# One transposition for the last 64 channels of two token tiles, two folded modulation vectors, and another order of the first operations

## The chip, the cores and the metric

The kernel runs on one core of one Trainium2 chip. The metric is the device time of one execution in microseconds, the median of several runs. The engines that a reader meets below are PE (TensorE, the matrix engine, with its weight loads listed apart as PEld), DVE (VectorE), ACT (ScalarE), POOL (GpSimd) and SP (SyncE, which here only issues loads and stores). Each engine runs its own instructions in program order and waits on semaphores for the others.

## The reference

The block has two halves. `x` is 2048 tokens of 448 channels. Six modulation vectors come from `silu(c) @ w_mod`.

```python
mod = (silu(c) @ w_mod).reshape(1, 6, 1, -1)
sa, ca, ga, sb, cb, gb = (mod[:, i] for i in range(6))
h = layernorm(x) * (1 + ca) + sa
qkv = h @ wqkv                       # 16 heads of 28 channels
pq, pk = phi(q), phi(k)              # phi(t) = where(t > 0, t + 1, exp(t)) + 1e-6
kv = einsum("bhsd,bhse->bhde", pk, v);  z = pk.sum(tokens)
num = einsum("bhqd,bhde->bhqe", pq, kv)
den = einsum("bhqd,bhd->bhq", pq, z)[..., None] + 1e-6
x = x + ga * ((num / den) @ wo)
h = layernorm(x) * (1 + cb) + sb
u = gelu(einsum("bsd,sf->bdf", h, w1) + b1)      # over tokens: 2048 -> 1792
x = x + gb * transpose(einsum("bdf,fs->bds", u, w2) + b2)
```

## The kernel before, in words

Tokens are cut into 16 tiles of 128, channels into three chunks of 128 and a last one of 64. Full precision is kept by splitting an operand into a high part (rounded, float32r) and a low part (the remainder): a product is hi x hi, hi x lo and lo x hi, three matmuls of 448 columns. The last chunk has only 64 rows, so its high and low parts lie one above the other in one operand of 128 rows. High parts are copies on ACT, low parts subtractions on DVE.

There is no scheduler: `tc.manual_schedule()` leaves the order of every engine's queue to the order of the calls in the source.

The stages, with the names that are used later:

- Start, about 0 to 22 us. SP issues the loads: transposed tiles `xt`, weights `wr`, the first two modulation weights `wt` (`wfirst`), tiles `x`. `keep_warm` gives PE matmuls on a constant, whose result nobody reads, until the first weights are there. `col_sum` (DVE) makes the scale (1 + ca) and the shift sa as columns; `w_high` and `w_low` make the weights with the scale folded in, `wh` and `wl`. `row_part` (DVE, tile `accb`) adds up the row bias that the shift gives, `row_sum` and `row_bias` (PE, bank `rowb`) sum it over partitions, and `row_out` writes it to the row operand `wrow`. The mean and variance of tiles 0 and 1 are made on ACT (`a_stats_act`, tile `as`) and finished on POOL (`mv`, `ve`, a power); those of later tiles begin on DVE. `a_rows` and `a_transpose` (`rowst`, bank `rw`) turn the means into a row of the moving operand. The projection `kp` of a tile is ended by `close`, one matmul with `wrow`.
- The loop for k and k^T x, t = 4 to 15, to about 100 us: projections `kp`, `a_exp` (`ek`, `rk`), `a_pk` (phi(k)), `a_pk_parts` (its high and low parts, and its sum over tiles, which a DMA issued by POOL accumulates), `a_outer` (banks `cacc`); some of the q projections are made early. The modulation vectors three to five are summed on DVE (`mod_part`), split (`mod_split`), and summed over partitions and spread by PE with a matrix of ones (`mod_sum2`, bank `modp`), 112 rows at a time.
- About 100 to 114 us: the sum of phi(k), kv, and its product with `wo` (`wp`), which is split into `Wph` and `Wpl`.
- The loop over token tiles, about 114 to 212 us, `for i in range(NT + LAG)`. In step i PE transposes phi(q)/den of tile i (`b_transpose`, `pn` to the bank `tq`), multiplies tile i - 1 (`b_out`, bank `op`, with the parts `pth` and `ptl` that `b_high`, `b_low` and `b_low_last` make of `tq`), and does the first twelve matmuls of the token MLP for tile i - 5 (`step`, banks `up`). DVE adds `op` to x (`b_res`, tile i - 2), prepares `pn` of tile i + 1 (`b_prod`, `b_sum`, `b_eps`, `b_recip`, `b_scale`), normalises and makes low parts.
- The rest of the token MLP, `up` to about 300 us and `y` to about 432 us.

Pools: 74 slots and 27 token slots of 512 columns in SBUF, 8 PSUM banks of 512 columns.

Of the kernel before, what the change touches and what calls it, by code (L numbers as in the profile page):

```python
# [8 lines left out]
F32 = mybir.dt.float32  # L9
# [5 lines left out]
P = 128  # L15
# [27 lines left out]
POOL_LOW = (0, 2)  # L43
PRE = 9
MID = 5
NSLOT, NTOK = 74, 27
# [5 lines left out]
def block_kernel(ctx: ExitStack, tc: tile.TileContext, x, xt, wqkv, wo, w1, b1, w2, b2, c, wmod, wfirst, out):  # L52
# [176 lines left out]


    def mod_split(j):
        acc = macc.pop(j)
        macc[j] = (moving(slot, f"mh{j}", parts=G), moving(slot, f"ml{j}", parts=G))
        split(acc, *macc[j])

    def mod_sum2(j):
        ps = bank(f"modp{j}")
        hi, lo = macc.pop(j)
        nc.tensor.matmul(ps[:, :D], ones_r[:G, :], hi, start=True, stop=False)
        nc.tensor.matmul(ps[:, :D], ones_r[:G, :], lo, start=False, stop=True)  # L240
        return ps
# [99 lines left out]
    def a_stats_act(ts):  # L341
        n = len(ts)
        g, ve = a_group(ts)
        sm = small.tile([P, n, 3], F32, name=f"as{ts[0]}", tag=f"as{n}")

        def one(i):
            t, s3 = ts[i], sm[:, i, :]
            nc.scalar.activation(junk, X[t], AF.Identity, accum_out=s3[:, 0:1])
            nc.scalar.activation(s3[:, 1:2], s3[:, 0:1], AF.Copy, scale=-1.0 / D)
            b_square(X[t], s3[:, 1:2], s3[:, 2:3], f"s{t}")  # L350

        def end():
            nc.gpsimd.tensor_scalar_mul(g[:, :, 0:1], sm[:, :, 0:1], 1.0 / D)
            nc.gpsimd.tensor_scalar(ve, sm[:, :, 2:3].to_broadcast([P, n, 2]), 1.0 / D, EPS,
                                    op0=ALU.mult, op1=ALU.add)
            a_pow(g, ve)
            groups[ts[0]] = g
        return one, end
# [137 lines left out]
    def a_pk_parts(t):  # L496
# [14 lines left out]
        pks[t] = (hi, lo)  # L511


    cacc = []
# [16 lines left out]
    spread()  # L531
    keep_warm(4)
    nc.scalar.activation(sel_s, sel_f, AF.Copy)
# [49 lines left out]
    end23()  # L583
    a_split_high(5)
    row_out(1)
    a_transpose(0)
    a_copy(0)
# [9 lines left out]
    load_xt(10)  # L597
    load_x(10)
    a_exp(0, kps[0])
    a_high(0)  # L600
# [20 lines left out]
    low()  # L621
    a_split(6)
    a_transpose(4)
# [18 lines left out]
    a_pk_parts(2)  # L642
    low()
    a_split(7)
    wo_sb = []
    late = [t for t in range(NT) if t not in Q_EARLY.values()]
    for t in range(4, NT):
# [53 lines left out]
        if pair:  # L701
            second(1)
            end()
        if 4 <= t < 8:
            w_high(0, t - 4)
            if t == 7:
                w_row(0)
# [82 lines left out]

    dens, prods = {}, {}

# [14 lines left out]
    def b_scale(t):  # L807
        pn = tslot(f"pn{t}")
        nc.vector.scalar_tensor_tensor(pn.rearrange("p (h d) -> p h d", d=DH),
                                       pq[t].rearrange("p (h d) -> p h d", d=DH), 1e-6,  # L810
# [5 lines left out]
    def b_transpose(t):  # L816
        pn = pns.pop(t)
        tps[t] = bank(f"tq{t}")
        for ch in range(3):
            nc.tensor.transpose(tps[t][:, ch * P:(ch + 1) * P], pn[:, ch * P:(ch + 1) * P], ident)  # L820
        nc.tensor.transpose(tps[t][:64, 384:], pn[:, 384:D], ident)
# [10 lines left out]
    def b_low_last(t):  # L832
        ps, hi = tps.pop(t), phs[t][0]
        nc.vector.tensor_sub(hi[64:, 384:], ps[:64, 384:], hi[:64, 384:].bitcast(F32))

    def b_out(t):
        ph, pl = phs.pop(t)
        opb[t] = bank(f"op{t}")
        todo = []
        for ch in range(3):  # L840
            s = slice(ch * P, (ch + 1) * P)
            todo += [(ph[:, s], Wph[ch]), (ph[:, s], Wpl[ch]), (pl[:, s], Wph[ch])]
        todo += [(ph[:, 384:], Wph[3]), (ph[:, 384:], Wpl[3])]
        for n, (a, b) in enumerate(todo):
            nc.tensor.matmul(opb[t][:, :D], a, b, start=(n == 0), stop=(n == len(todo) - 1))  # L845

# [85 lines left out]
    for i in range(NT + LAG):  # L932
# [4 lines left out]
        if i == NT:  # L937
            mod_split(5)
        if i < NT:
            b_transpose(i)  # L940
# [376 lines left out]
```

## Time and profile before

| | |
|---|---|
| Time, median of 3 runs | 437.97 us (437.96 to 438.0) |
| Profiled execution | 438.01 us |
| Its span | 436.3 us |
| Instructions | 7203 |
| PE busy | 429.2 us (98%) |
| DVE busy | 360.6 us (83%) |
| ACT busy | 275.3 us (63%) |
| POOL busy | 117.9 us (27%) |

The span is the time from the first to the last instruction in the trace; the execution around it is 1.7 us longer. In the rows that are quoted below, "kp<-wh,hh" names the output and the inputs of an instruction, "128x448" its elements (partitions x columns), x3 how often it stands there; a group of rows with the same line, engine and shape can be one row. Times that matmuls end are modelled, so consecutive matmuls overlap in the rows and their pitch is the distance of their starts.

### The profile page before, as it was taken

How to read it: one execution, taken by the hardware profiler on the slowest of the kernel's cores; microseconds unless marked ns; L12 is line 12 of the kernel's file. 1: busy time of each engine (PE TensorE's matmuls, PEld its weight loads, DVE VectorE, ACT ScalarE, POOL GpSimd, SP SyncE). 2: the span in 40 equal slices, each digit the busy share in tenths (PEclk: the TensorE clock that was granted, in tenths of full speed). 3: DMA queues.
4: the chain of work that ended last, by engine and by line, in shares of the span. 5: the costliest groups of instructions: out<-in, count | busy, mean ns of one | idle time of the engine just before them, and what ended most of it. 6: DMA issues, size and time to landing. Idle time of an engine off the chain costs nothing.

```text
span 436.3 us, 7203 instructions
## 1 busy us (share of the span) xinstructions
PE 429.2 (98%) x2337; PEld 398.8 (91%) x2337; DVE 360.6 (83%) x809; ACT 275.3 (63%) x587; POOL 117.9 (27%) x200
## 2 busy tenths in 40 slices
PE   8899999999999999999999999999999999999996
PEld 8688899999899999999999999999999999999996
DVE  4899986689799999994679695829799988898894
ACT  5689867749657798886756263537464565645550
POOL 4335454100024477773300000010113131132010
PEclk9999999999999999999999999999999999999999
DMA  8997998465300036335417561587379977985430
GB/s 273 382 338 154 228 230 200 80 193 180 124 2 0 26 66 152 74 74 139 152 65 223 178 209 45 148 213 218 71 171 235 201 173 156 223 180 119 83 54 32
DMA packets 63941, 66.14 MB, mean 152 GB/s; under 512 B 4960, under 2 KB 55456, under 8 KB 63904
## 3 DMA queue, kind: packets, MB, share of 16 engines
q1 hardware_dynamic: 54832, 50.90, 37.6%
q0 software_dynamic: 8784, 14.32, 20.9%
q10 hardware_dynamic: 288, 0.46, 0.5%
q8 instruction: 18, 0.29, 0.3%
q14 instruction: 19, 0.16, 0.1%
HBM read 46.30 MB, written 7.34 MB: 123 GB/s over the span
## 4 chain that ended last, share of the span: by engine, by line
PE 89%; DVE 3%; DMA 2%; ACT 2%; POOL 1%; issue 1%; SPq 1%; DVEq 0%; ACTq 0%; POOLq 0%
PE y L1112 19%; PE up L897 10%; PE up L896 10%; PE up L895 10%; PE y L1113 9%; PE op L845 8%; PE qp L419 7%; PE cacc L525 6%; PE kp L419 3%; PE tq L820 1%; DMA wr<-in_qkv_dram 1%; DMA x<-in_A_x_dram 1%; PE qp L426 1%; PE kvb L776 1%; DVE st L367 1%
## 5 line engine op out<-in xcount | busy, mean ns | idle before, releaser
L896 PE MATMUL up<-h2l,ph 128*128 128x448 f32 x224 | 81.3, 363 | 0.0
L897 PE MATMUL up<-h2h,pl 128*128 128x448 f32 x224 | 81.2, 363 | 0.0
L895 PE MATMUL up<-h2h,ph 128*128 128x448 f32 x224 | 80.8, 361 | 0.0
L1067 POOL DMA_DIRECT2D a<-a x16 | 14.2, 959 | 138.0 <-DMA a<-in_B_w_dram 77.1
L896 PEld LDWEIGHTS up<-h2l,ph 128*128 128x128 f32 x224 | 42.0, 188 | 3.3 <-DVE h2l L892 0.3
L895 PEld LDWEIGHTS up<-h2h,ph 128*128 128x128 f32 x224 | 41.9, 187 | 3.0
L897 PEld LDWEIGHTS up<-h2h,pl 128*128 128x128 f32 x224 | 42.0, 188 | 2.5
L84 DVE TENSOR_TENSOR pl<-pr,ph 128x512 fp32r<-128x512 f32 x46 | 30.7, 685 | 4.2 <-ACT ph L83 3.3
L1118 ACT ACTIVATE cc<-y 128x448 f32<-128x448 f32 x24 | 13.0, 547 | 26.8 <-PE y L1113 26.8
L83 ACT ACTIVATE ph<-pr 128x512 fp32r<-128x512 f32 x46 | 27.6, 625 | 0.8 <-PE up L897 0.5
L1031 DVE TENSOR_TENSOR u<-u,mod 128x448 f32<-128x448 f32 x14 | 8.7, 621 | 21.6 <-ACT u L1030 21.4
L419 PE MATMUL kp<-wh,hh 128*128 128x448 f32 x64 | 24.4, 386 | 0.2 <-ACT rk L436 0.2
L845 PE MATMUL op<-wph,pth 128*128 128x448 f32 x64 | 24.5, 383 | 0.0
L1030 ACT ACTIVATE u<-up,b1c 128x448 f32<-128x448 f32 x14 | 8.8, 627 | 24.0 <-PE up L897 23.5
L1132 POOL DMA_DIRECT2D out_dram<-yt x14 | 12.7, 910 | 40.5 <-DVE yt L1123 31.1
L525 PE MATMUL cacc<-pkh,xh 128*128 128x448 f32 x64 | 23.6, 369 | 0.0
L419 PE MATMUL qp<-wh,hh 128*128 128x448 f32 x64 | 23.4, 366 | 0.0
L845 PE MATMUL op<-wpl,pth 128*128 128x448 f32 x64 | 23.1, 361 | 0.0
L802 POOL TENSOR_SCALAR den<-den 128x16 f32<-128x16 f32 x16 | 8.8, 549 | 43.6 <-DVE den L799 43.6
L525 PE MATMUL cacc<-pkl,xh 128*128 128x448 f32 x56 | 20.3, 362 | 0.0
L1073 DVE TENSOR_TENSOR a<-a,s 128x512 f32<-128x512 f32 (+1 forms) x32 | 18.5, 619 | 0.0
L1112 PE MATMUL y<-ub,a11h 128*128 128x448 f32 x56 | 18.2, 375 | 0.0
(233 smaller groups left out, 1362.3 us busy)
## 6 DMA issues: line engine op xcount, KB each, us to landing
pr<-in_B_w_dram SPq DMA_DIRECT2D x56, 256.0 KB, 3.0
a<-in_B_w_dram SPq DMA_DIRECT2D x32, 256.0 KB, 4.6
a<-in_B_w_dram SPq DMA_DIRECT2D x32, 192.0 KB, 4.6
xt<-in_xt_dram SPq DMA_DIRECT2D x16, 256.0 KB, 5.0
x<-in_A_x_dram SPq DMA_DIRECT2D x16, 224.0 KB, 5.0
wm<-in_B_wmod_dram SPq DMA_DIRECT2D x16, 196.0 KB, 4.9
out_dram<-x SPq DMA_DIRECT2D x14, 224.0 KB, 2.4
out_dram<-yt POOLq DMA_DIRECT2D x14, 224.0 KB, 5.5
```

The source lines that it names most:

```text
L83: nc.scalar.activation(hi, full, AF.Copy)
L84: nc.vector.tensor_sub(lo, full, hi.bitcast(F32))
L419: nc.tensor.matmul(pps[t, j][:, :D], a[:, ch * P:(ch + 1) * P], w, start=first, stop=False)
L525: nc.tensor.matmul(cacc[ch][:, :D], a[:, s], b, start=(t == 0 and i == 0), stop=(t == NT - 1 and i == len(todo) - 1))
L845: nc.tensor.matmul(opb[t][:, :D], a, b, start=(n == 0), stop=(n == len(todo) - 1))
L895: nc.tensor.matmul(ps[:, :D], hi[:, sl], mh, start=first, stop=False)
L896: nc.tensor.matmul(ps[:, :D], hi[:, sl], ml, start=False, stop=False)
L897: nc.tensor.matmul(ps[:, :D], lo[:, sl], mh, start=False, stop=last)
L1067: nc.gpsimd.dma_start(w, a, accum_op=ALU.add)
L1073: nc.vector.tensor_tensor(w, raw2[q, a][i], raw2[q, b][i], op=op)
L1112: nc.tensor.matmul(ps[:, :D], h[:, s], w, start=opens and r == 0, stop=False, skip_group_check=True)
L1113: nc.tensor.matmul(ps[:, :HD], l[:, s], wh, start=False, stop=closes and r == PAIRS - 1, skip_group_check=True)
```

## The change

It has four parts.

**Transposition.** `pn` gets a slot of 512 columns. The transposition of an even tile leaves out its last 64 channels; ACT copies them beside the last 64 of the next tile (`b_beside`), and the odd tile's fourth transposition turns both at once, 128 columns. High and low parts of the last chunk of both tiles are then made in the odd step, across partitions where needed. The two matmuls of an even tile with its last chunk (`b_out_last`) move to the start of the step after the next one, ahead of its transposes.

PE in the loop over token tiles, before: the end of a step and the next one (ph and pl are parts of W1, h2h and h2l of the normalised tile).

```order
L897 MATMUL up3_1924<-h2h1_1952,pl1_1350 128x448
L820 MATMUL tq7_2062<-ident_78,pn7_2049 128x128 x3
L821 MATMUL tq7_2062<-ident_78,pn7_2049 64x128
L845 MATMUL op6_2067<-wph0_1610,pth6_2012 128x448
...
L845 MATMUL op6_2067<-wph3_1622,pth6_2012 128x448
L845 MATMUL op6_2067<-wpl3_1623,pth6_2012 128x448
L895 MATMUL up0_1921<-h2h2_2027,ph2_1396 128x448
...
L897 MATMUL up3_1924<-h2h2_2027,pl2_1397 128x448
L820 MATMUL tq8_2138<-ident_78,pn8_2125 128x128 x3
```

And after, the step of tile 8 and the beginning of that of tile 9:

```order
L937 MATMUL up3_1922<-h2h2_2029,pl2_1399 128x448
L885 MATMUL op6_2067<-wph3_1622,pth6_2013 128x448
L885 MATMUL op6_2067<-wpl3_1623,pth6_2013 128x448
L848 MATMUL tq8_2140<-ident_78,pn8_2125 128x128 x3
L878 MATMUL op7_2144<-wph0_1610,pth7_2089 128x448
...
L885 MATMUL op7_2144<-wpl3_1623,pth7_2089 128x448
...
L937 MATMUL up3_1922<-h2h3_2101,pl3_1403 128x448
L848 MATMUL tq9_2212<-ident_78,pn9_2171 128x128 x4
```

The last two matmuls of op6 now stand behind the up matmuls of the step before and ahead of the transposes of tile 8; the odd tile has four whole transposes.

DVE in the same loop, after, from the parts of tile 7 to those of tile 8 (before, each tile had one L834 row, the low part of its own last chunk, between L805 and L809):

```order
L863 TENSOR_TENSOR ptl7_2090<-tq7_2062,pth7_2089 128x384
L831 RECIPROCAL den8_2111<-den8_2111 128x16
L870 TENSOR_TENSOR pth6_2013<-tq7_2062,pth6_2013 64x128
L870 TENSOR_TENSOR pth7_2089<-tq7_2062,pth7_2089 64x128
L835 SCALAR_TENSOR_TENSOR pn8_2125<-pq8_1683,den8_2111 128x448
L932 TENSOR_TENSOR h2l3_2102<-y3_2037,h2h3_2101 128x448
L894 SCALAR_TENSOR_TENSOR x6_170,sm6_2173<-op6_2067,x6_170 128x448
L821 SCALAR_TENSOR_TENSOR pd9_2175<-pq9_1685,zb_1380 128x448
...
L863 TENSOR_TENSOR ptl8_2169<-tq8_2140,pth8_2168 128x384
L831 RECIPROCAL den9_2190<-den9_2190 128x16
L835 SCALAR_TENSOR_TENSOR pn9_2171<-pq9_1685,den9_2190 128x448
```

The two low parts of the last chunks of tiles 6 and 7 stand together ahead of pn8; the residual sum of tile 6 stands where it stood, and its op6 now ends two matmuls into PE's step of tile 8.

**Folding.** For the third and sixth modulation vectors (j = 2 and 5) DVE first adds the upper 48 of the 112 rows to the lower ones; the 64 rows that are left are split into a high and a low half of one operand of 128 rows, and PE needs one matmul instead of two.

**Start.** `x` of tile 0 is issued ahead of the four loads of the first modulation weights and `x` of tile 1 between them; `keep_warm` runs seven instead of four; the column sums and row parts alternate, without the low part of tile 3 between them; the mean and variance of tiles 0 and 1 are finished on DVE (their power stays on POOL); the low part of tile 4 stands behind `wrow`, and the high part of tile 6 ahead of the first exponential.

DVE in the start, before, from the first column sum of the shift (wt_0_138) to wrow's predecessors:

```order
L220 SCALAR_TENSOR_TENSOR wt_0_138,col_202<-wt_0_138,scr 128x449
L220 SCALAR_TENSOR_TENSOR wt_1_141,col_202<-wt_1_141,scr 128x449
L220 SCALAR_TENSOR_TENSOR wt_2_144,col_202<-wt_2_144,scr 128x449
L220 SCALAR_TENSOR_TENSOR wt_3_147,col_202<-wt_3_147,scr 64x449
L265 TENSOR_SCALAR accb_309<-wr_0_117,col_202 128x448
L402 TENSOR_TENSOR hl_301<-xt_154,hh_300 128x512
L267 SCALAR_TENSOR_TENSOR accb_309<-wr_1_122,col_202,accb_309 128x448
L267 SCALAR_TENSOR_TENSOR accb_309<-wr_2_129,col_202,accb_309 128x448
L267 SCALAR_TENSOR_TENSOR accb_309<-wr_3_134,col_202,accb_309 128x448
L402 TENSOR_TENSOR hl_316<-xt_156,hh_315 128x512
L382 CAST rowst_104<-mv_282 128x4x2
```

And after:

```order
L222 SCALAR_TENSOR_TENSOR wt_0_140,col_202<-wt_0_140,scr 128x449
L222 SCALAR_TENSOR_TENSOR wt_1_143,col_202<-wt_1_143,scr 128x449
L282 TENSOR_SCALAR accb_293<-wr_0_117,col_202 128x448
L284 SCALAR_TENSOR_TENSOR accb_293<-wr_1_122,col_202,accb_293 128x448
L222 SCALAR_TENSOR_TENSOR wt_2_148,col_202<-wt_2_148,scr 128x449
L222 SCALAR_TENSOR_TENSOR wt_3_151,col_202<-wt_3_151,scr 64x449
L284 SCALAR_TENSOR_TENSOR accb_293<-wr_2_129,col_202,accb_293 128x448
L284 SCALAR_TENSOR_TENSOR accb_293<-wr_3_134,col_202,accb_293 128x448
L370 TENSOR_SCALAR mv_285<-as_287 128x2
L371 TENSOR_SCALAR ve_286<-as_287 128x4
L419 TENSOR_TENSOR hl_315<-xt_154,hh_314 128x512
L399 CAST rowst_104<-mv_285 128x4x2
```

The low part of tile 3 (hl of xt_154) has left the row parts, mv and ve have come behind them, and the low part of tile 4 (hl of xt_156) is no longer ahead of rowst.

**Sums.** The DMA that adds phi(k) of a tile to the running sum is issued at the end of the step (`sum_end`), behind the statistics' power on POOL and not ahead of it.

The diff, cut:

```diff
+FOLDED = (2, 5,)
...
     load_xt(2)
+    load_x(0)
     for ch in range(4):
+        if ch == 2:
+            load_x(1)
         load_first(0, ch)
-    load_x(0)
-    load_x(1)
...
+    def halves(acc, new, name):
+        n = acc.shape[0] - 64
+        nc.vector.tensor_add(acc[:n], acc[:n], acc[64:])
+        both = moving(new, name)
+        nc.scalar.activation(both[:64], acc[:64], AF.Copy)
+
+        def low():
+            nc.vector.tensor_sub(both[64:], acc[:64], both[:64].bitcast(F32))
+        return both, low
...
     def mod_sum2(j):
         ps = bank(f"modp{j}")
-        hi, lo = macc.pop(j)
-        nc.tensor.matmul(ps[:, :D], ones_r[:G, :], hi, start=True, stop=False)
-        nc.tensor.matmul(ps[:, :D], ones_r[:G, :], lo, start=False, stop=True)
+        part = macc.pop(j)
+        for i, m in enumerate(part):
+            nc.tensor.matmul(ps[:, :D], ones_r[:m.shape[0], :], m, start=(i == 0), stop=(i == len(part) - 1))
         return ps
...
         def end():
-            nc.gpsimd.tensor_scalar_mul(g[:, :, 0:1], sm[:, :, 0:1], 1.0 / D)
-            nc.gpsimd.tensor_scalar(ve, sm[:, :, 2:3].to_broadcast([P, n, 2]), 1.0 / D, EPS,
+            nc.vector.tensor_scalar_mul(g[:, :, 0:1], sm[:, :, 0:1], 1.0 / D)
+            nc.vector.tensor_scalar(ve, sm[:, :, 2:3].to_broadcast([P, n, 2]), 1.0 / D, EPS,
...
         elif t in SUM_DMA:
-            nc.gpsimd.dma_start(pksum[t % 2], pk, accum_op=ALU.add)
+            late_sum.append((pksum[t % 2], pk))
...
-    keep_warm(4)
+    keep_warm(7)
...
-    for ch in range(4):
+    for ch in (0, 2):
         col_sum(0, ch)
+        col_sum(0, ch + 1)
+        row_part(1, ch)
+        row_part(1, ch + 1)
     row_sum(1)
-    a_split_high(3)
     act01(1)
     end01()
-    row_part(1, 0)
-    a_split_low(3)
-    for ch in (1, 2, 3):
-        row_part(1, ch)
-    a_split(4)
+    a_split(3)
     projects(in_turn(3)[:4], 1, "kp")
     row_bias(1)
     projects(in_turn(3)[4:], 1, "kp")
+    a_split_high(4)
+    a_split_high(5)
...
-    a_split_high(5)
     row_out(1)
+    a_split_low(4)
...
+    a_split_high(6)
     a_exp(0, kps[0])
...
     def b_transpose(t):
         pn = pns.pop(t)
         tps[t] = bank(f"tq{t}")
-        for ch in range(3):
+        if t % 2 == 0:
+            lasts[t] = pn
+        for ch in range(3 + t % 2):
             nc.tensor.transpose(tps[t][:, ch * P:(ch + 1) * P], pn[:, ch * P:(ch + 1) * P], ident)
-        nc.tensor.transpose(tps[t][:64, 384:], pn[:, 384:D], ident)
+
+    def b_beside(t):
+        pns[t + 1] = tslot(f"pn{t + 1}", w=512)
+        nc.scalar.activation(pns[t + 1][:, D:], lasts.pop(t)[:, 384:D], AF.Copy)
 
     def b_high(t):
...
-        nc.scalar.activation(phs[t][0][:64, 384:], tps[t][:64, 384:], AF.Copy)
+        if t % 2:
+            for i, s in ((t, slice(0, 64)), (t - 1, slice(64, P))):
+                nc.scalar.activation(phs[i][0][s, 384:], tps[t][s, 384:], AF.Copy)
...
     def b_low_last(t):
-        ps, hi = tps.pop(t), phs[t][0]
-        nc.vector.tensor_sub(hi[64:, 384:], ps[:64, 384:], hi[:64, 384:].bitcast(F32))
+        ps = tps.pop(t)
+        if t % 2:
+            for i, s, o in ((t - 1, slice(64, P), slice(0, 64)), (t, slice(0, 64), slice(64, P))):
+                hi = phs[i][0]
+                nc.vector.tensor_sub(hi[o, 384:], ps[s, 384:], hi[s, 384:].bitcast(F32))
...
+    def b_out_last(t):
+        ph = phs.pop(t)[0]
+        for b in (Wph, Wpl):
+            nc.tensor.matmul(opb[t][:, :D], ph[:, 384:], b[3], start=False, stop=(b is Wpl))
...
+        if i % 2 == 0 and 0 < i <= NT:
+            b_out_last(i - 2)
         if i < NT:
             b_transpose(i)
...
             b_high(i)
+            if i % 2 == 0:
+                b_beside(i)
```

More of the change, by code (lines that the diff above doesn't have):

```diff
@@ L228, in mod_part @@
             nc.vector.scalar_tensor_tensor(macc[j], wm[j, k], sc[:G, k:k + 1], macc[j], op0=ALU.mult, op1=ALU.add)
+    def halves(acc, new, name):
[6 more added lines that the diff above has]
+        return both, low
     def mod_split(j):
         acc = macc.pop(j)
-        macc[j] = (moving(slot, f"mh{j}", parts=G), moving(slot, f"ml{j}", parts=G))
-        split(acc, *macc[j])
+        if j in FOLDED:
+            both, low = halves(acc, slot, f"mh{j}")
+            low()
+            macc[j] = (both,)
+        else:
+            macc[j] = (moving(slot, f"mh{j}", parts=G), moving(slot, f"ml{j}", parts=G))
+            split(acc, *macc[j])
     def mod_sum2(j):
         ps = bank(f"modp{j}")
-        hi, lo = macc.pop(j)
-        nc.tensor.matmul(ps[:, :D], ones_r[:G, :], hi, start=True, stop=False)
-        nc.tensor.matmul(ps[:, :D], ones_r[:G, :], lo, start=False, stop=True)
+        part = macc.pop(j)
+        for i, m in enumerate(part):
+            nc.tensor.matmul(ps[:, :D], ones_r[:m.shape[0], :], m, start=(i == 0), stop=(i == len(part) - 1))
         return ps
@@ L511, in a_pk_parts, with sum_end @@
         pks[t] = (hi, lo)
+    late_sum = []
+    def sum_end():
+        while late_sum:
+            nc.gpsimd.dma_start(*late_sum.pop(0), accum_op=ALU.add)
     cacc = []
@@ L621, in block_kernel @@
     low()
-    a_split(6)
+    a_split_low(6)
     a_transpose(4)
@@ L643, in block_kernel @@
     low()
+    sum_end()
     a_split(7)
@@ L703, in block_kernel @@
             end()
+        sum_end()
         if 4 <= t < 8:
@@ L789, in block_kernel @@
     pns, phs, ys, opb, sums, nms, nm2s, rss, vss = {}, {}, {}, {}, {}, {}, {}, {}, {}
-    dens, prods = {}, {}
+    dens, prods, lasts = {}, {}, {}
     def b_prod(t):
@@ L807, in b_scale @@
     def b_scale(t):
-        pn = tslot(f"pn{t}")
-        nc.vector.scalar_tensor_tensor(pn.rearrange("p (h d) -> p h d", d=DH),
+        pn = pns.pop(t, None) or tslot(f"pn{t}", w=512)
+        nc.vector.scalar_tensor_tensor(pn[:, :D].rearrange("p (h d) -> p h d", d=DH),
                                        pq[t].rearrange("p (h d) -> p h d", d=DH), 1e-6,
@@ L832, in b_low_last @@
     def b_low_last(t):
-        ps, hi = tps.pop(t), phs[t][0]
-        nc.vector.tensor_sub(hi[64:, 384:], ps[:64, 384:], hi[:64, 384:].bitcast(F32))
+        ps = tps.pop(t)
[3 more added lines that the diff above has]
+                nc.vector.tensor_sub(hi[o, 384:], ps[s, 384:], hi[s, 384:].bitcast(F32))
     def b_out(t):
-        ph, pl = phs.pop(t)
+        ph, pl = phs[t]
         opb[t] = bank(f"op{t}")
-        todo = []
         for ch in range(3):
             s = slice(ch * P, (ch + 1) * P)
[L842 to L845, printed above, removed]
+            for n, (a, b) in enumerate(((ph[:, s], Wph[ch]), (ph[:, s], Wpl[ch]), (pl[:, s], Wph[ch]))):
+                nc.tensor.matmul(opb[t][:, :D], a, b, start=(ch == n == 0), stop=False)
+        if t % 2:
+            b_out_last(t)
+    def b_out_last(t):
+        ph = phs.pop(t)[0]
+        for b in (Wph, Wpl):
+            nc.tensor.matmul(opb[t][:, :D], ph[:, 384:], b[3], start=False, stop=(b is Wpl))
     def b_sums(i):
```

## The prediction

> **What bounds the kernel now.** I read the page first, then TensorE's waits, then the chain of the first 45 us, then the timelines of the two places that the change touches. The page's lines on busy time and on the granted clock:
>
> ```profile
> span 436.3 us, 7203 instructions
> PE 429.2 (98%) x2337; PEld 398.8 (91%) x2337; DVE 360.6 (83%) x809; ACT 275.3 (63%) x587; POOL 117.9 (27%) x200
> PEclk9999999999999999999999999999999999999999
> ```
>
> TensorE (PE) is busy for 98% of the span, at an open clock in every slice. So a matmul taken away is worth its pitch, and other engines cost something only where PE waits. TensorE's whole list of waits has five rows; four matter (us in total, times, longest):
>
> ```profile
> PE rowb L277 <- DVE accb L267: 1.6, 1, 1.6
> PE kp L426 <- DVE wrow L282: 0.5, 1, 0.5
> PE kp L419 <- ACT rk L436: 0.2, 1, 0.2
> PE rw L391 <- DVE rowst L385: 0.2, 1, 0.2
> ```
>
> That is 2.5 us. The chain of waits shows where (start, us, engine):
>
> ```profile
> 9.02 4.84 DMA x<-in_A_x_dram
> ...
> 16.12 0.57 ACT junk L348 x2
> ...
> 17.79 0.43 POOL ve L354
> 18.29 1.50 POOL mv L339
> ...
> 21.58 0.64 DVE wrow L282
> 22.35 0.46 PE kp L426
> ...
> 43.56 0.32 PE rw L391
> ```
>
> All PE idleness lies before 43.6 us; from there to the end the chain is PE alone. The change has then two kinds of gain: fewer matmuls anywhere, and shorter waits in the first 44 us. And one kind of loss: new waits in a stretch that has none.
>
> **The transposes.** PE around two steps of the loop over token tiles:
>
> ```profile
> 163.02 0.49 PE L820 MATMUL tq<-ident,pn 128*128 128x128 f32 x3
> 163.35 0.27 PE L821 MATMUL tq<-ident,pn 128*64 128x128 f32 x1
> 168.07 0.49 PE L820 MATMUL tq<-ident,pn 128*128 128x128 f32 x3
> ```
>
> Three transposes advance PE by 163.35 - 163.02 = 0.33 us, 0.11 each; the step is 5.05 us long. A pair of tiles has 8 transposes before and 7 after, so 8 fewer in all: 8 x 0.11 = 0.88 us. The other bound comes from their loads (nanoseconds, min/median/max):
>
> ```profile
> L820 PEld LDWEIGHTS tq<-ident,pn x48: 139/141/146, 113.7 to 193.4; 128*128 128x128 f32 x48
> L821 PEld LDWEIGHTS tq<-ident,pn x16: 109/111/111, 114.3 to 193.5; 128*64 128x64 f32 x16
> ```
>
> Sixteen loads of 111 ns give way to eight of 141: 1.78 - 1.13 = 0.65 us. I take 0.88, since the pitch of 0.11 is shorter than either load and so the loads don't set it. The Trainium skill, "TensorE: Matmul & The Clock Gate", section "LDWEIGHTS (loading the stationary operand)", speaks against the edit: a load costs by its columns alone, so eight of 128 columns cost as much as sixteen of 64, and were loads the limit the term would be zero and the sum 436.5. The rows above differ from it, 111 to 141 ns and not one to two.
>
> What the edit adds off PE: one ACT copy (128x64) per pair, and on DVE both low parts of the last chunk in the odd step. DVE:
>
> ```profile
> 161.07 0.28 DVE L834 TENSOR_TENSOR pth<-tq,pth 64x128 fp32r<-64x128 f32 x1
> 161.38 0.62 DVE L809 SCALAR_TENSOR_TENSOR pn<-pq,den 128x448 f32<-128x448 f32 x1
> 162.46 0.62 DVE L854 SCALAR_TENSOR_TENSOR x<-op,x 128x448 f32<-128x448 f32 x1
> 166.32 0.63 DVE L809 SCALAR_TENSOR_TENSOR pn<-pq,den 128x448 f32<-128x448 f32 x1
> ```
>
> DVE's step is 166.32 - 161.38 = 4.94 us, with no idle time: it is only 0.11 shorter than PE's. After the change a pair costs PE 2 x 5.05 - 0.11 = 9.99 and DVE 9.88. The cover is thin, and here lies the new wait: the residual sum (b_res, L854) of an even tile needs the two last matmuls of its output, which now stand at the start of PE's step two later. In the rows b_res starts at 162.46, 0.56 before PE's step at 163.02. After, it can start at the earliest 0.66 us into that step (a pitch of 0.2, a matmul of 0.36, and 0.1 as my estimate for the hand-over). Queued behind b_res on DVE are all other steps of the tile, pn included, for which PE's next transposes wait. So DVE falls back once by 0.56 + 0.66 = 1.2 us against PE. It had pn ready at 161.38 + 0.62 = 162.0 for a transpose at 163.02: 1.0 us of reserve, less 0.3 where two low parts (161.07 to 161.38 is one) stand ahead of pn. That leaves a stall between 0 and 0.6 us, when the reserve is first used up; I take 0.25, less than the middle, because even steps of DVE are shorter by the same 0.3. Does it repeat? From the low parts to the next b_res DVE has pn and the low part of h2 to do (161.38 to 162.46, 1.09 us), and the last matmuls need 0.66 beside them. So the round trip is 9.88 - 1.09 + 0.66 = 9.45 us, less than PE's 9.99: it should not repeat. Net: -0.63 us (-0.88 to -0.05).
>
> **The folds.** ACT, DVE and PE around the third modulation vector:
>
> ```profile
> 70.07 0.56 ACT L83 ACTIVATE mh<-acc 112x448 fp32r<-112x448 f32 x1
> 72.09 0.64 ACT L436 ACTIVATE rk<-kp,mv 128x448 f32<-128x448 f32 x1
> ```
> ```profile
> 71.13 0.63 DVE L84 TENSOR_TENSOR ml<-acc,mh 112x448 fp32r<-112x448 f32 x1
> ```
> ```profile
> 74.97 0.36 PE L239 MATMUL modp<-mh,ones_r 112*128 112x448 f32 x1
> 75.17 0.36 PE L240 MATMUL modp<-ml,ones_r 112*128 112x448 f32 x1
> ```
>
> One matmul of two goes, 75.17 - 74.97 = 0.2 us, for each of two vectors: -0.4 us. The price is one more DVE addition, and that ACT now waits for it: DVE reaches this place at 71.13, so the copy starts near 71.7 and not at 70.07, and ACT's queue behind it is 1.6 us late. The low half is then ready near 72.9, two us ahead of its matmul. The relu (72.09 + 0.64) ends at 74.4 and not 72.7; the projection that takes over its bank stands behind modp, at 75.2: 0.8 us of cover. If it were gone, PE would lose what is over, at most 1.6 - 0.8. For the sixth vector the copy stands in steps in which ACT has time; I cost it at nothing.
>
> **The start.** TensorE:
>
> ```profile
> 3.19 0.85 PE L184 MATMUL warm<-ones 128*128 128x128 f32 x3
> ...
> 6.33 2.08 PE L184 MATMUL warm<-ones 128*128 128x128 f32 x8
> 8.06 0.72 PE L419 MATMUL kp<-wh,hh 128*128 128x448 f32 x1
> ...
> 9.32 0.57 PE L419 MATMUL kp<-wh,hh 128*128 128x448 f32 x1
> 9.70 0.40 PE L419 MATMUL kp<-wh,hl 128*128 128x448 f32 x1
> 9.94 0.36 PE L419 MATMUL kp<-wh,hh 128*128 128x448 f32 x1
> ```
>
> Four warming matmuls are eight passes, 1.73 us to 8.06, 0.216 each. Three more cost 6 x 0.216 = 1.3 us: projections begin at 9.35. The clock opens at 9.7 (the pitch falls from 0.38 to 0.24 and below); if it opens then again, two projections have started by 9.94 and not five, so PE is 3 x 0.2 = 0.6 us behind. It has 1.62 us of waiting to hide that in. DVE and ACT:
>
> ```profile
> 12.29 0.62 DVE L220 SCALAR_TENSOR_TENSOR wt<-wt,scr 128x449 f32<-128x449 f32 x1
> ...
> 14.46 0.44 DVE L265 TENSOR_SCALAR accb<-wr,col 128x448 f32<-128x448 f32 x1
> 16.15 0.69 DVE L402 TENSOR_TENSOR hl<-xt,hh 128x512 fp32r<-128x512 f32 x1 [1.25 <-ACT hh L398]
> 16.76 2.12 DVE L267 SCALAR_TENSOR_TENSOR accb<-wr,col,accb 128x448 f32<-128x448 f32 x3
> ```
> ```profile
> 13.88 0.58 ACT L348 ACTIVATE junk<-x 128x448 f32<-128x448 f32 x1 [1.75 <-DMA x<-in_A_x_dram]
> ```
> ```profile
> DMA packets 817, 1.34 MB, mean 395 GB/s; under 512 B 89, under 2 KB 664, under 8 KB 817
> ```
>
> The low part of tile 3 (L402, with 1.25 us of waiting) no longer stands inside the row bias: accb is done at 12.29 + 2.17 + 0.44 + 2.12 = 17.0 and not 18.9. PE arrives at 18.93 - 1.62 + 0.6 = 17.9, so the first wait goes. The moved loads: at 395 GB/s (the answer for 6 to 9.4 us) a load of 224 KB takes 0.57 us, so x0, no longer behind four, lands at 13.88 - 4 x 0.57 = 11.6; the statistics can begin when ACT is free, 13.88 - 1.75 = 12.1. Two tiles of 1.67 (16.12 to 17.79) end at 15.4. The two loads that are put back by x0 and x1 come one or two places later, for column sums that are also later by the two row parts. Mean and variance now stand on DVE behind accb: 17.0 plus two small instructions, 0.2 to 0.6, I take 0.25. The pow, 1.50, starts at 17.25 and not 18.29. What follows it up to wrow and the closing matmul moves along: 22.35 - 1.04 = 21.3. PE, at 17.9, has 22.35 - 18.93 - 0.49 = 2.9 us of work up to there: it arrives at 20.8 and waits 0.5 still. So the wait is shortened by 1.0 us, not 2.1.
>
> The low part of tile 4 (0.69 as in L402's row) is moved behind wrow, between 0 and 0.7 us on DVE's chain; after it PE was not waiting, and I cost it at 0. The high part of tile 6, made before the first exponential, takes away the 0.2 wait for rk. The sums of phi(k) are now issued on POOL behind the pow, which the rw wait of 0.2 hangs on; the sums come later by that pow, and nothing but a later sum takes them. Start: -1.0 - 0.2 - 0.2 = -1.4 us (0 to -2.5, which is all of PE's waits; the 0.6 alone is no loss, since 1.62 covers it).
>
> **Sum.** -1.4 - 0.63 - 0.4 = -2.4. The profiled execution took 438.01 us, 1.7 more than its span and 0.04 more than the median of 437.97. 438.0 - 2.4 = 435.6, for the median as well.
>
> **Rivals.**
> - The clock opens later, since warming matmuls in place of projections don't hold it open. For it speaks that the pitch fell 1.6 us after the projections began; against it, that PE was busy from 3.19 on, mostly with the same warming work. How much later can't be read: between 0 and 9.70 - 3.19 = 6.5 us. At the middle, 3.3 us, PE does 9 projections and not 16 or 17 in it, 7.6 x 0.2 = 1.5 us lost beyond the 0.6; PE reaches the row bias at 19.4, the close at 22.3, and the 1.0 is gone; with the two small waits 438.0 - 0.4 - 0.63 - 0.4 = 436.6. [...]
> - The reordered start does nothing: the moved x loads or the column sums come late (the queue is full at 395 GB/s), and the close stays at 22.35, as do the small waits. Then only matmuls are saved: 438.0 - 0.63 - 0.4 = 437.0, or 437.3 with the stall at its upper bound.
> - Slower: DVE becomes the bound of the token loop through b_res. It decides when the round trip passes 9.99 plus what was gained: over some six pairs in which PE has nothing else to do, 2.4 us of gain are used up at 9.99 + 2.4 / 6 = 10.4 us, 0.95 above my 9.45. For it speaks that DVE has no idle time and that the hand-over crosses PE, DVE and PE in order; against it, that 0.66 hides beside 1.09. At a round trip of 10.8 it loses 6 x 0.8 = 4.8 and gives 435.6 + 4.8 - 0.6 = 439.8.
> - More is gained: no stall, and both waits at the start gone: 438.0 - 2.5 - 0.9 - 0.4 = 434.2.
>
> **How the numbers follow.** A difference of 0.2%, 0.9 us, is about what a measurement can tell from none. The forecast, 435.6 with a range of 434.8 to 436.1 of its own, 0.58; the late clock 0.15; the idle reorder 0.12, more than half of it inside 0.2% if a stall goes with it; slower 0.10; more gain 0.05. So faster 0.82, same 0.08, slower 0.10. A range of 434.4 to 437.3 leaves out the slower case and some of the gain.
>
> **What would show it.** Right: transposes 56, all 128x128, and one modp matmul for the third and sixth vectors; the wait of rowb for accb gone, and the closing matmul near 21.3 us with a wait of about 0.5; the pitch of projections falling at 9.7; steps of the token loop 9.99 us a pair, DVE's b_res of even tiles just behind the last op matmuls, and at most one PE wait for pn there, about 0.25. Wrong: the full pitch only after 11 us; x statistics of ACT not before 13 us; PE waits for pn or low parts in several pairs; or an ACT wait near 71 us that shows up as a PE wait behind modp.

## The result, and the profile after

The changed kernel takes 436.03 us (median of 5 runs, 435.97 to 436.23), the kernel before 438.00 in the same comparison: a ratio of 0.9954 with a 95% interval of 0.9941 to 0.9968. That is 2.0 us less, inside the forecast range and 0.4 short of the forecast 435.6.

The page of the changed kernel, busy time by engine:

```profile
span 434.3 us, 7208 instructions
PE 428.0 (99%) x2333; PEld 395.3 (91%) x2333; DVE 362.4 (83%) x813; ACT 278.7 (64%) x595; POOL 118.6 (27%) x198
```

PE's waits after the change (us in total, times, longest):

```profile
PE kp L443 <- DVE wrow L299: 0.8, 1, 0.8
PE kp L436 <- DVE wl L276: 0.4, 1, 0.4
PE rw L408 <- DVE rowst L402: 0.2, 1, 0.2
PE tq L848 <- DVE pn L835: 0.2, 1, 0.2
```

The wait of `rowb` for `accb` (1.6) and that of `kp` for `rk` (0.2) are gone. So is the wait of `rw` at 43.6 us: the 0.2 in this list is another, at 19.4. The wait ahead of the closing matmul has grown from 0.5 to 0.8, and two are new, one in the token loop and one of 0.4 for `wl` at 9.7 us. The second costs nothing that shows: in the lists of four experiments it is absent, and the closing matmul still waits 0.8 there. Where the 2.0 us come from is read by looking up the same matmul in both timelines. After:

```profile
21.11 0.65 PE L443 MATMUL kp<-wrow,hl 98*128 98x448 f32 x2 [0.76 <-DVE wrow L299]
...
73.18 0.36 PE L443 MATMUL qp<-wrow,hl 98*128 98x448 f32 x1
73.39 0.36 PE L257 MATMUL modp<-mh,ones_r 128*128 128x448 f32 x1
73.59 0.36 PE L436 MATMUL kp<-wh,hh 128*128 128x448 f32 x1
...
112.31 0.49 PE L848 MATMUL tq<-ident,pn 128*128 128x128 f32 x3
...
201.14 0.36 PE L257 MATMUL modp<-mh,ones_r 128*128 128x448 f32 x1
201.34 0.36 PE L935 MATMUL up<-h2h,ph 128*128 128x448 f32 x1
```

And before:

```profile
74.76 0.37 PE L426 MATMUL qp<-wrow,hl 98*128 98x448 f32 x1
...
114.07 0.49 PE L820 MATMUL tq<-ident,pn 128*128 128x128 f32 x3
...
202.94 0.37 PE L239 MATMUL modp<-mh,ones_r 112*128 112x448 f32 x1
...
203.36 0.36 PE L895 MATMUL up<-h2h,ph 128*128 128x448 f32 x1
```

| Place | Before | After | Gain up to there | Of which here |
|---|---|---|---|---|
| closing matmul of tile 0 | 22.35 | 21.11 | 1.24 | 1.24 |
| qp closed, ahead of the first fold | 74.76 | 73.18 | 1.58 | 0.34 |
| first transpose of the token loop, behind that fold | 114.07 | 112.31 | 1.76 | 0.18 |
| the second fold, behind the token loop's transposes | 202.94 | 201.14 | 1.80 | 0.04 |
| the matmul behind the second fold | 203.36 | 201.34 | 2.02 | 0.22 |

So the start gave 1.6 us, each fold its 0.2, and the token loop, from which the forecast expected 0.63, nothing. Its steps show why. PE around tiles 8, 14 and 15 after the change:

```profile
155.54 0.36 PE L885 MATMUL op<-wpl,pth 128*128 128x448 f32 x1
156.07 0.52 PE L848 MATMUL tq<-ident,pn 128*128 128x128 f32 x3 [0.17 <-DVE pn L835]
...
166.09 0.38 PE L848 MATMUL tq<-ident,pn 128*128 128x128 f32 x2
...
176.08 0.49 PE L848 MATMUL tq<-ident,pn 128*128 128x128 f32 x3
...
185.87 0.36 PE L885 MATMUL op<-wpl,pth 128*128 128x448 f32 x1
186.24 0.52 PE L848 MATMUL tq<-ident,pn 128*128 128x128 f32 x3
...
191.01 0.37 PE L937 MATMUL up<-h2h,pl 128*128 128x448 f32 x1
191.47 0.63 PE L848 MATMUL tq<-ident,pn 128*128 128x128 f32 x4
```

From 166.09 to 176.08 a pair takes 9.99 us, the forecast's number (10.09 to 10.10 before). But at three places a transpose starts later than the usual 0.2 us after the matmul ahead of it: by 0.33 us (155.54 to 156.07), 0.17 (185.87 to 186.24) and 0.26 (191.01 to 191.47), 0.76 in all. The list of waits names only a part of the first. DVE over the same stretch and a little ahead of it:

```profile
133.93 0.62 DVE L894 SCALAR_TENSOR_TENSOR x<-op,x 128x448 f32<-128x448 f32 x1 [0.32 <-PE op L885]
...
145.93 0.62 DVE L894 SCALAR_TENSOR_TENSOR x<-op,x 128x448 f32<-128x448 f32 x1 [0.96 <-PE op L885]
...
155.29 0.62 DVE L835 SCALAR_TENSOR_TENSOR pn<-pq,den 128x448 f32<-128x448 f32 x1
...
180.91 0.46 DVE L228 TENSOR_SCALAR acc<-wm,sc 112x448 f32<-112x448 f32 x1
...
185.47 0.62 DVE L835 SCALAR_TENSOR_TENSOR pn<-pq,den 128x448 f32<-128x448 f32 x1
...
186.55 0.68 DVE L230 SCALAR_TENSOR_TENSOR acc<-wm,sc,acc 112x448 f32<-112x448 f32 x1
...
190.69 0.63 DVE L835 SCALAR_TENSOR_TENSOR pn<-pq,den 128x448 f32<-128x448 f32 x1
```

The residual sum of tile 2 waits 0.32 us for the two last matmuls of its output at 133.9, and that of tile 4 waits 0.96 at 145.9. `pn` of tile 8 is then ready only just ahead of its transposes (155.29 + 0.62 = 155.91, for 156.07), and for the tiles 9 to 13 the reserve is 0.3 to 0.6 us, where before it was 1.0 to 1.4. Near the end DVE also adds up the sixth modulation vector (the `acc` rows), and `pn` of tiles 14 and 15 is late again. In the kernel before, the same additions took the reserve down to 0.7 us at tile 15 (192.00 + 0.62 = 192.62, for 193.30), and no stall came of it:

```profile
192.00 0.62 DVE L809 SCALAR_TENSOR_TENSOR pn<-pq,den 128x448 f32<-128x448 f32 x1
```
```profile
193.30 0.49 PE L820 MATMUL tq<-ident,pn 128*128 128x128 f32 x3
```

That is a reading; the experiments test it.

### The profile page after: what moved, and what is told of

It reads as the page before. It is cut to its first block, busy times and chain, and to the rows that moved or that the text cites. A ratio compares the mean times of both kernels' runs of the same rounds, so it can differ in the third digit from the quotient of the medians.

```text
span 434.3 us, 7208 instructions
## 1 busy us (share of the span) xinstructions
PE 428.0 (99%) x2333; PEld 395.3 (91%) x2333; DVE 362.4 (83%) x813; ACT 278.7 (64%) x595; POOL 118.6 (27%) x198
## 4 chain that ended last, share of the span: by engine, by line
PE 92%; DVE 4%; DMA 2%; issue 1%; POOL 0%; ACT 0%; SPq 0%; DVEq 0%
PE y L1156 19%; PE up L935 10%; PE up L937 10%; PE up L936 10%; PE y L1157 9%; PE cacc L548 8%; PE qp L436 7%; PE op L878 6%; PE kp L436 5%; PE tq L848 1%; PE op L885 1%; DMA wr<-in_qkv_dram 1%; PE kp L443 1%; DMA xt<-in_xt_dram 1%; PE qp L443 1%; PE kvb L802 1%
## 5 line engine op out<-in xcount | busy, mean ns | idle before, releaser
L878 PE MATMUL op<-wph,pth 128*128 128x448 f32 x48 | 18.7, 389 | 0.0
L84 ACT ACTIVATE s2h<-s 128x512 fp32r<-128x512 f32 (+1 forms) x16 | 8.3, 569 | 15.5 <-DVE s L1117 15.5
```

Of the source, the lines that this page charges most:

```text
L84: nc.scalar.activation(hi, full, AF.Copy)
L878: nc.tensor.matmul(opb[t][:, :D], a, b, start=(ch == n == 0), stop=False)
```

## The experiments

Times are medians of 5 to 11 runs beside the kernel before on the same chip, which took 437.99 to 438.04. "The changed kernel" means 436.03; it was measured in a comparison of its own, beside 438.00.

**The token loop: does the shared transposition gain anything?** The transposition was undone in the changed kernel, and put alone into the kernel before. Of the diff, only its transposition part was reverted or applied:

```diff
-        for ch in range(3 + t % 2):
+        for ch in range(3):
             nc.tensor.transpose(tps[t][:, ch * P:(ch + 1) * P], pn[:, ch * P:(ch + 1) * P], ident)
...
+        nc.tensor.transpose(tps[t][:64, 384:], pn[:, 384:D], ident)
...
-        if i % 2 == 0 and 0 < i <= NT:
-            b_out_last(i - 2)
```

> The changed kernel with the transposition of the kernel before (four transposes in every tile), all else as changed. Theory A, from the two traces: in the token loop the saved transposes (0.8 us) are given back in three stalls before tiles 8, 14 and 15 (0.33, 0.17 and 0.26 us), so undoing them costs nothing: 436.0, and no PE stall between 112 and 200 us. Theory B, the forecast's term of -0.63 us for the loop: 436.6 to 436.7.

> The kernel before with the shared transposition alone. Theory A: the stalls come back, as they belong to the loop and not to the start: 438.0 less 0.1 at most. Theory B: 437.4.

Undone: 436.03 us, exactly the changed kernel's time, and its steps are 5.05 us with no stall. Alone: 437.98, exactly the time before (a ratio of 0.9999, 0.9990 to 1.0008), with the same stalls, of 0.33, 0.20 and 0.26 us. PE in the kernel with the transposition alone, ahead of tile 8:

```profile
157.17 0.36 PE L859 MATMUL op<-wpl,pth 128*128 128x448 f32 x1
157.70 0.52 PE L822 MATMUL tq<-ident,pn 128*128 128x128 f32 x3 [0.17 <-DVE pn L809]
```

This part of the change is worth nothing as it stands, with either start. The 0.8 us that the transposes save are given back in the stalls.

**What makes the two late stalls?** The four DVE additions of the sixth modulation vector were moved to where no later transposition waits for DVE:

```diff
-        if NT - 3 <= i <= NT:
-            mod_part(5, i - NT + 3)
+        for k in {NT - 1: (0, 1), NT: (2, 3)}.get(i, ()):
+            mod_part(5, k)
```

> The changed kernel, with the four additions of the sixth modulation vector on DVE not in the steps 13 to 16 but two each in the steps 15 and 16, after the last transposition has its input. If the stalls before tiles 14 and 15 come from these additions (0.4 and 0.6 us each, in a loop whose reserve the residual sum had used up), they vanish and the time falls by 0.43 us to 435.6; the stall of 0.33 before tile 8 stays. If they come from the round trip between the residual sum and the last matmuls, nothing changes: 436.0.

435.66 us. PE ahead of tiles 14 and 15:

```profile
186.24 0.36 PE L885 MATMUL op<-wpl,pth 128*128 128x448 f32 x1
186.44 0.49 PE L848 MATMUL tq<-ident,pn 128*128 128x128 f32 x3
...
191.18 0.37 PE L937 MATMUL up<-h2h,pl 128*128 128x448 f32 x1
191.38 0.60 PE L848 MATMUL tq<-ident,pn 128*128 128x128 f32 x4
```

Both transposes now follow after 0.20 us. The stall before tile 8 stays, at 0.34. So these additions, which a reserve had covered before, are what was late there.

**What took the reserve?** The residual sum of an even tile was put behind two other DVE operations of its step:

```diff
-        if res and i < NT + 1:
+        held = res and i < NT + 1 and i % 2 == 0
+        if res and i < NT + 1 and not held:
             b_res(i - 2)
         if scale:
             b_prod(i + 1)
+        if held:
+            if norm1:
+                b_norm1_a(i - 3)
+            b_res(i - 2)
...
-        if norm1:
+        if norm1 and not held:
             b_norm1_a(i - 3)
```

> The changed kernel, with the residual sum of an even tile on DVE behind two other operations of its step (the product for the next tile's denominators and the first normalisation), 1.1 us later in the queue. If the hand-over from the last two matmuls to this sum set DVE back (it waits 0.96 us once at 145.9 us and 0.3 once more), the wait goes, DVE keeps its reserve and all three stalls vanish: 435.3. If DVE is too slow in itself for the shorter steps, the stalls stay: 436.0.

435.20 us, and no stall is left in the loop, though the additions stand where they stood. From its first transpose to the second fold the loop takes 88.01 us (112.27 to 200.28) and not 88.87 as before the change: 0.86 us, the worth of the saved transposes when no stall takes it back. DVE's longest wait for the last matmuls:

```profile
145.90 0.62 DVE L894 SCALAR_TENSOR_TENSOR x<-op,x 128x448 f32<-128x448 f32 x1 [0.35 <-PE op L885]
```

0.35 us and not 0.96, and the wait at tile 2 is gone. The hand-over from PE to the residual sum is the cause: DVE is fast enough for the shorter steps, but lost its lead in these two waits.

**The start: where do mean and variance belong?** They were put back on POOL:

```diff
-            nc.vector.tensor_scalar_mul(g[:, :, 0:1], sm[:, :, 0:1], 1.0 / D)
-            nc.vector.tensor_scalar(ve, sm[:, :, 2:3].to_broadcast([P, n, 2]), 1.0 / D, EPS,
+            nc.gpsimd.tensor_scalar_mul(g[:, :, 0:1], sm[:, :, 0:1], 1.0 / D)
+            nc.gpsimd.tensor_scalar(ve, sm[:, :, 2:3].to_broadcast([P, n, 2]), 1.0 / D, EPS,
```

> The changed kernel with mean and variance of tiles 0 and 1 finished on POOL again, as in the kernel before. In the changed kernel's trace ACT has the sums ready at 15.4 us, but mv and ve stand on DVE behind accb and start at 16.8. Theory A: on POOL they start at 15.5 and take 0.7, the pow starts near 16.2 and not at 17.1, all behind it follows, and PE's wait of 0.76 us ahead of the closing matmul goes: 435.3. Theory B, the change's order is worth its 1.0 us also for this part: POOL's two small operations are slower than DVE's, the closing matmul comes later by 0.4 or more: 436.4.

435.15 us (435.02 to 436.33), 0.9 less than the changed kernel. The changed kernel on ACT, DVE and POOL:

```profile
15.22 0.19 ACT L344 ACTIVATION_READ_ACCUMULATOR junk<-x,as 128x1 f32 x1
```
```profile
15.51 1.39 DVE L284 SCALAR_TENSOR_TENSOR accb<-wr,col,accb 128x448 f32<-128x448 f32 x2
16.82 0.16 DVE L370 TENSOR_SCALAR mv<-as 128x2 f32<-128x2 f32 x1
```
```profile
17.13 1.41 POOL L356 TENSOR_TENSOR mv<-ve,roots 128x4 f32<-128x4 f32 x1 [3.76 <-DVE ve L371]
```

And this experiment on POOL, and PE's closing matmul:

```profile
15.23 0.74 POOL L371 TENSOR_SCALAR ve<-as 128x4 f32<-128x4 f32 x1 [0.79 <-ACT junk L344]
16.05 1.49 POOL L356 TENSOR_TENSOR mv<-ve,roots 128x4 f32<-128x4 f32 x1
```
```profile
20.11 0.64 PE L443 MATMUL kp<-wrow,hl 98*128 98x448 f32 x2 [0.48 <-DVE wrow L299]
```

POOL takes 0.74 us for the variance, DVE 0.16; but POOL is idle when the sums are ready, and DVE is in the row bias for another 1.4 us. The pow starts at 16.05 and not 17.13, and the closing matmul comes 1.0 us sooner. Of that, 0.26 belongs to this one execution, in which ACT had its sums ready, ahead of the moved operations, at 15.15 and not at 15.41. From there to the closing matmul it is 4.96 us here and 5.70 in the changed kernel. So this part of the change costs 0.7 us by the traces, 0.9 by the medians, and the rest of the new start gains more than the whole of it showed.

**Does the number of warming matmuls matter?**

```diff
-    keep_warm(7)
+    keep_warm(4)
```

> The changed kernel with four warming matmuls instead of seven. Theory A: they only fill time in which PE would wait later, so nothing changes: 436.0, with a wait of rowb or of the closing matmul up by the same 0.6 us. Of the clock: in the profiles with seven it opened at 4.7 to 5.7 us, in the two with four at 9.8 and 10.6. If the number of warming matmuls does that, it opens near 10 here; if it is the phase of each run, it can open at either place. Theory B, the late clock costs what the forecast's rival said: 437.

436.23 us (435.88 to 436.30): no difference that the runs tell from the changed kernel. The wait is found at another place than expected: PE waits 0.4 us for `wh` at its first projection, and still 0.8 ahead of the closing matmul. The reverse edit, seven in the kernel before:

> The kernel before with seven warming matmuls and nothing else. Time: 438.0, as PE's wait for accb covers what they cost. Clock: it opened at 9.8 and 10.6 us in the two profiles with before's start and at 4.2 to 5.9 in the eight with the changed start, four warming matmuls in one of them. If it is the phase of the run, it can open at either place here; near 10 says that something else in the start is behind it.

438.09 us against 438.04: no difference either. PE waits 1.0 us for `accb` there and not 1.6. That alone does not show the forecast's cover at work, for the kernel with the transposition alone has four warming matmuls and waits 1.1. What the two share is a clock that opened later than the 9.8 us of the kernel before, at 10.2 and 10.6: a PE that comes later waits less.

**Are the folds worth their matmuls?**

```diff
-FOLDED = (2, 5,)
+FOLDED = ()
```

> The changed kernel without the folds. One matmul of 0.2 us comes back twice and nothing else on TensorE: 436.4. If the later ACT queue near 70 us cost anything in the changed kernel, less than that: 436.0.

436.48 us, 0.45 more than with the folds. The ACT queue that they delay costs nothing.

**Can the rest of the wait at the closing matmul go?** `row_out`, which makes `wrow`, was called ahead of the second tile's statistics:

```diff
     low()
+    row_out(1)
     first23(1)
     second23(0)
     second23(1)
     end23()
-    row_out(1)
```

> The changed kernel with wrow on DVE ahead of the second tile's statistics, the two aggregations and the variance (1.07 us in the trace). Its other input, ACT's copy, is ready at 18.9, so wrow can start at 19.3 and not at 20.3. The closing matmul then waits for ACT's copies into hl, which end at 20.4: it comes at 20.4 and not at 21.1, a gain of 0.65 us: 435.4. If the delayed statistics of tiles 2 and 3 (0.6 us later) are what PE needs next, the gain comes back as a wait of rw or of kp: 436.0.

436.06 us: the second theory. PE:

```profile
22.89 0.32 PE L408 MATMUL rw<-ident,rowst 128*98 128x128 f32 x1 [0.43 <-DVE rowst L402]
```

The closing matmul did come without a wait, at 20.02 (20.4 expected). But the statistics of tiles 2 and 3 are then later, and the next transposition of means waits for them at 22.89; in the changed kernel it starts at 23.04. Of 1.1 us only 0.15 is left, and the runs don't show it.

**The moved loads.**

```diff
     load_xt(2)
+    for ch in range(4):
+        load_first(0, ch)
     load_x(0)
-    for ch in range(4):
-        if ch == 2:
-            load_x(1)
-        load_first(0, ch)
+    load_x(1)
     load_xt(3)
```

> The changed kernel with the x loads of tiles 0 and 1 behind the four first modulation weights again. By the forecast's working the statistics end 2.2 us later, at 17.6 and not 15.4, and mean and variance on DVE then wait for them and not for accb (16.8): the pow starts at 17.9 and not at 17.1, and the closing matmul comes 0.8 us later: 436.8. If accb, earlier by its loads, is what counts, no change: 436.0.

436.57 us, 0.54 more (436.33 to 436.77, and one run of 438.20), near the expected number but by another way. PE in this experiment:

```profile
6.57 3.25 PE L185 MATMUL warm<-ones 128*128 128x128 f32 x14
9.58 0.45 PE L435 MATMUL kp<-wh,hh 128*128 128x448 f32 x1
...
17.55 0.47 PE L435 MATMUL kp<-wh,hh 128*128 128x448 f32 x1 [0.30 <-ACT hh L414]
...
21.14 0.73 PE L442 MATMUL kp<-wrow,hl 98*128 98x448 f32 x2
...
30.57 0.37 PE L547 MATMUL cacc<-pkh,xh 128*128 128x448 f32 x1
31.01 0.47 PE L547 MATMUL cacc<-pkh,xl 128*128 128x448 f32 x1
```

The closing matmul comes at 21.14, without a wait, and in the changed kernel at 21.11: up to there next to nothing is lost. The statistics did come later (ACT's second ends at 16.98 and not at 15.4), but only as late as `accb` (16.99), so mean and variance didn't wait. What the later statistics hold up is ACT's queue behind them. PE waits 0.30 us at 17.55 for `hh`, the next high part on ACT; the same matmul starts at 16.20 in the changed kernel. ACT's first exponential then comes at 22.02 and not at 21.65, and `xl` on DVE at 30.40 and not at 30.08. PE starts its first matmul with this `xl` 0.44 us after the one ahead of it (30.57 to 31.01), in the changed kernel 0.24 (30.44 to 30.68). From there on this trace is 0.3 to 0.4 us behind, and its execution took 436.34, 0.37 more than the changed kernel's profiled one. This is a reading of one trace that no further run tests.

PE's clock opened late in this trace. Its warming ran at 0.215 us a pass ((9.58 - 6.57) / 14) and its projections began at 9.58; in the changed kernel a pass takes 0.114 us ((7.19 - 5.60) / 14), and the clock was open before 5.6 us. But even so PE had done all that stood ahead by 17.25 and stood idle until 17.55, so what the late clock cost lies behind the wait for `hh`, and the run shows no price of its own for it.

**The small waits of the start.** The DMA for the sums of phi(k) was issued ahead of the pow again, and the high part of tile 6 put back:

```diff
-            late_sum.append((pksum[t % 2], pk))
+            nc.gpsimd.dma_start(pksum[t % 2], pk, accum_op=ALU.add)
...
-    a_split_high(6)
     a_exp(0, kps[0])
...
-    a_split_low(6)
+    a_split(6)
...
```

> The changed kernel with the sums of phi(k) issued ahead of the pow again and the high part of tile 6 in its old place. By the forecast the two waits of 0.2 us (kp for rk, rw for rowst) come back: 436.4. If DVE's and ACT's shifted queues have made room, nothing comes back: 436.0.

436.46 us (435.89 to 436.62). One wait is back in PE's list:

```profile
PE kp L436 <- ACT rk L453: 0.2, 1, 0.2
```

The other, of `rw` behind the pow at 42 us, is not in the list, but the timeline has it:

```profile
41.49 0.37 PE L542 MATMUL cacc<-pkl,xh 128*128 128x448 f32 x1
42.01 0.32 PE L408 MATMUL rw<-ident,rowst 128*98 128x128 f32 x1
```

The transposition follows after 0.52 us, and in the changed kernel after 0.20 (41.86 to 42.06). From the closing matmul to the first closed qp this trace takes 39.11 us (20.76 to 59.87), the changed kernel's 38.68: the two waits together cost 0.43, as expected. This execution took only 436.05, because it had its closing matmul 0.35 us sooner, ahead of the edit. The runs scatter by 0.7 us, so the size rests on the trace.

**Both gains together.** The residual sum later, and the statistics on POOL:

> The changed kernel with both edits that helped alone: the residual sum of an even tile 1.1 us later on DVE, and mean and variance of tiles 0 and 1 on POOL. They act in different stretches, 16 to 21 us and 145 to 192 us, so if each gain is its own they add: 436.0 - 0.8 - 0.9 = 434.3. If an earlier start only uses up reserve in the token loop, less: 434.8 to 435.2.

434.67 us, a ratio of 0.9923 to the kernel before (0.9910 to 0.9937), faster than both kernels. The two alone gave 0.83 and 0.88, together 1.36; its runs reach from 434.12 to 435.21, so that the sum, 434.3, is within them. By the traces nothing is lost in the token loop: from the closing matmul to the second fold it is 179.15 us (20.45 to 199.60), 0.88 less than in the changed kernel. The start gives 0.66 there (20.45 for 21.11), close to the 0.7 that the traces gave it alone.

## Why the prediction was right, and where its sum was off

- **The bound.** Right: with PE at 98%, what changed the time is found again as PE's work or PE's waits. Edits that took something from PE and gave it back as a wait further on, the transposition as it stands and `wrow` first, showed nothing.
- **Saved transposes.** Right in size: 10.09 to 9.99 us a pair, and 0.86 us for the loop without stalls (0.88 forecast, 0.65 if loads set the pitch). So loads of 128 columns for loads of 64 did not set the pitch, and the zero that the forecast drew from the Trainium skill did not come.
- **The hand-over to the residual sum.** This is the term that was mis-sized. The mechanism was right: DVE falls back (by 0.32 and 0.96 us at two residual sums, 1.28 in all; 1.2 was worked out, for one), the first stall comes when the reserve is used up (0.33 measured, 0.25 taken, 0 to 0.6 the bounds), and the round trip does not repeat it (9.99 from tile 9 to tile 13). What failed is the last step, that nothing else needed the reserve. The forecast read DVE's step from one place, 4.94 us, and did not ask what DVE has to do in the steps 13 to 16. There the sixth modulation vector adds 0.4 to 0.6 us a step, and without a reserve that is 0.43 more in stalls. The trace of the kernel before had the sign of it, the reserve of only 0.7 us at tile 15. The loop gained 0.04 us and not 0.63.
- **Folds.** Right: 0.18 and 0.22 in the traces, 0.45 by the experiment without them. The cover near 70 us held.
- **The start.** Right in sum (1.58 for 1.4), and close in its steps: `accb` at 16.8 (17.0), first statistics at 12.0 (12.1), pow at 17.13 (17.25), closing matmul at 21.11 (21.3), a wait left there of 0.76 (0.5). The two small waits were worth 0.34 by the table and 0.43 by the experiment (0.4). Two steps were not right. The clock did not open at 9.7 us but before 5.6, so PE came sooner and waited longer for `wrow`; and the move of mean and variance to DVE was counted inside a gain while it is a loss of 0.7 to 0.9. The forecast priced it where the change had put it, behind `accb`, and did not work out the other place.
- **The late clock.** This rival asked for a clock later than before; it opened earlier instead. In the experiment with the loads back, seven warming matmuls and projections from 9.58, the closing matmul came at 21.14 and not at the rival's 22.3. No run had the changed start and a clock later than before, so the rival's price is not tested.
- **The slower rival.** It did not come: the round trip stayed below PE's pair. Its sum has a -0.6 for which the forecast gives no source.
- **Readings.** Two were off and left the 435.6 as it is. PE's warming does not begin at 3.19 us; that row is the end of a group from 1.11 on, so the upper bound for the late clock was 9.70 - 1.11 = 8.6 us and not 6.5. The profile's clock row reads open in its first slice, to 10.9 us, though the pitch falls only at 9.7: the trace's first record of a granted clock is at 9.77.
- **Luck.** 436.03 lies just inside the forecast's own 434.8 to 436.1. The loop gave 0.59 us less than forecast and the start 0.18 more, and the second is chance: the start holds a loss of 0.7 to 0.9 that the forecast did not see, and gains that it did not see either make up for it.

## What to carry to other kernels

When a change makes one engine wait for another, the cost is not only the stall that follows at once: it uses up the lead of the waiting engine's whole queue, and every later extra in that queue (here four additions, from 35 us further on) can then show as a stall of the engine that is the bound. So look at the step in which the waiting engine has most to do, not at the usual one. A wait for a result that has just moved can be cured by the order of the consumer's queue: here two operations drawn ahead of the residual sum gave the transposes' gain back. And an idle slow engine can be the better place for a small operation than a fast one with a queue: 0.74 us on POOL at once were worth more than 0.16 on DVE 1.4 us later.

## What the runs showed of the hardware that was not expected

The clock's opening, told by the pitch of the warming passes and first projections and by the first granted clock that each trace records, fell in two groups. In the ten profiles with x of tiles 0 and 1 loaded early it came between 4.2 and 6.1 us; in the four with the old order of loads (the kernel before, the transposition alone, seven warming matmuls alone, the loads put back) between 9.6 and 10.6. The number of warming matmuls does not divide them: four stand in both groups, and seven too. PE's first operations are the same in both groups. In each of the ten profiles the clock had opened before the first moved load was issued (at 4.67 and 5.99 us in the changed kernel), so these loads did not open it. The order of loads goes together with the opening, and why is open. The Trainium skill, "TensorE: Matmul & The Clock Gate", section "What's actually happening", has windows that run freely, whose phase then differs from run to run; a division by the order of loads does not follow from that, and no run here tried one kernel in several profiles.
